# Weight sums of a four-layer attention and SwiGLU kernel as queued steps, in a ring of three groups, with all norms' powers on GpSimd

## The chip, the core and the metric

The kernel runs on one core of a Trainium2 chip. The metric is the device time of one execution in microseconds, and the median of several runs is compared. The kernel before takes 1567.19 us (median of three runs, 1566.94 to 1567.77).

The engines carry the profile's names: PE is TensorE (PEld its weight loads), DVE is VectorE, ACT is ScalarE, POOL is GpSimd, and SP is SyncE, which here only issues transfers. Each engine executes its own instructions strictly in the order in which the program lists them; an instruction that waits for another engine holds up everything behind it.

## The reference

Input x has 2048 tokens of 1024 channels in bfloat16. Two kinds of layer alternate, each twice, and the two layers of a kind share their weights:

```
x = x + A(layernorm(x), wqkv, wo)    # 32 heads of 32; each token attends to 8 tokens, 2 apart, backwards
x = x + B(layernorm(x), w1, w3, w2)  # h = silu(xn @ w1) * (xn @ w3);  out = h @ w2;  F = 3584
x = x + A(...)
x = x + B(...)
```

Layernorm has no weights: (x - mean) / sqrt(var + 1e-5).

## The kernel before

**Units and stages.** The tokens are cut into four chunks of 512. A unit is one chunk in one of the two passes, so there are eight units. First the q, k and v products of the first pass are made for all four chunks (`q_part`), with the attention's scores and values on VectorE beside them. Then `b_stage(u, ...)` runs for each unit: the SwiGLU layer of that chunk, and from unit 1 on also the next pass's q, k and v products of a later chunk.

**Two ways to compute the SwiGLU layer.** Units 0 and 1 (`u < TU`, with `TU = 2`) use ordinary matmuls. The 28 column blocks of F are handled in two splits (16 and 12 blocks), and in groups of four blocks: a group needs one tile of w1 and one of w3, each [128, 8, 512] in bfloat16, 1 MB. For each block, eight matmuls make a gate tile `pg` in PSUM (L1224), ScalarE takes it through Silu to `sg` (L1228), eight more make the up tile `pu` (L1233), and VectorE multiplies the two into `hT` (L1237). After a split comes its w2 stage: eight output tiles `acc` (L1253), added to x by VectorE (L1263). Units 2 to 7 use a seven-product scheme (`products`, L1104 and L1039) that multiplies sums of weight blocks in float16. It spares matmuls, but it needs those sums.

**The weight sums.** They are made once, during units 0 and 1, beside the ordinary matmuls: unit 0 makes those of w1, unit 1 those of w3, and each unit makes half of w2's. For one group of w1 or w3, seven in each unit:

- `measure` (L856): ScalarE squares the whole tile and sums the squares; the squares themselves go to a scratch tile `junk`.
- `scales` (L870): a one-column float32 matmul with a matrix of ones adds the sums over the partitions; four small VectorE steps (L861 to L865) make a power of two out of that.
- `copies` (L883): for each half `a` of the group, four scaled ScalarE copies into a sums buffer. There are two sums buffers, one for each half, both in the tile `big`.
- `differences` (L894): four VectorE subtractions; then GpSimd issues two stores to DRAM (`t_d`, L896 and L897). The buffer is free when those have landed.

`prepare` puts these pieces at fixed places of a group: it is called after each gate tile and each up tile, eight slots in all. Slot 0 measures, slot 4 scales, slots 5 and 7 copy. Parts of w2 go through `transform2` (copies L967, subtractions L972, store L974) at every second output tile of the w2 stage. The sizes of w2 are taken earlier, by `measure2` during the first q, k and v products.

**What sets the order.** The program lists instructions in an order that a planner in the kernel's own code works out while it is built. It keeps a clock for each engine (`now`) and estimates of durations: 0.216 us for a matmul of 512 columns, 7.0 us from the end of the subtractions to a free sums buffer, and for a load 0.45 us of issue, 0.2 us, its kilobytes over 380 and 1.3 us. VectorE's background work lies in queues (`norms`, `makes`, `adds`, `values`, `scores`). `background(until)` lists those steps that fit before a given time. `act_background` does the same for ScalarE with the queues `acts` and `reads`; it takes a step if it would end no later than 2.2 us past TensorE's clock. Small matmuls that wait for VectorE go to `pe_queue`. `pe_requests` takes one when TensorE's clock is 1.5 us past the time at which it is due. `between` calls it once per block.

**The ring.** Weight tiles sit in a ring of six slots of 1 MB (pool `wp`). `seq` lists what goes into them in order, `load_weight` issues the load for the next entry, and `release(n)` with `flush` lets n more entries in. In units 0 and 1 a group takes three entries: w1, w3 and `junk`, which is never loaded. So the ring holds the present group and the next. A group's slots are released when its matmuls are listed (`release(3)` at the group's end).

**The norms.** For the chunks that VectorE normalizes, `norm_stats` takes mean and variance (L233, L236), ScalarE takes Sqrt of the variance (L238, ten times), and VectorE takes its reciprocal (L269) and applies it (L261). For the others `act_norm` does the work on ScalarE, with the power -0.5 on GpSimd (L318 to L324). The ScalarE functions Sqrt, Silu and Exp lie in different tables, and a change of function costs an ACT_TABLE_LOAD.

Of the kernel before, what the change touches and what calls it, by code (L numbers as in the profile page):

```python
# [7 lines left out]
FP32 = mybir.dt.float32  # L8
# [9 lines left out]
def kernel(  # L18
# [186 lines left out]
    nc.gpsimd.memset(ones[:], 1.0)  # L205
    size = const.tile([P, 2, NG], FP32, name="size")
    up_scale = const.tile([P, 2, NG], FP32, name="up_scale")
# [18 lines left out]
    def norm_stats(key, c, r):  # L226

        st = small.tile([P, 2, 2, 6], FP32, name="st")
        mv = small.tile([P, 2, 2], FP32, name="mv", bufs=4)
        sd = small.tile([P, 2], FP32, name="sd", bufs=4)  # L230

        def stats(i, hh):
            nc.vector.bn_stats(st[:, i, hh, :], x_sb[:, c * TPC + 2 * r + i, hh * 512:(hh + 1) * 512])  # L233

        def aggregate(i):
            nc.vector.bn_aggr(mv[:, i, :], st[:, i, :, :])  # L236
            if i == 1:
                nc.scalar.activation(sd[:], mv[:, :, 1], ACTF.Sqrt, bias=epst[:])  # L238
                moments[key, r] = mv, sd, act(0.3, now["dve"] + 0.1, "sqrt")

        for i in range(2):
            for hh in range(2):
                yield 0.61, x_at[c], lambda: stats(i, hh)
            yield 0.12, 0.0, lambda: aggregate(i)

    def norm_apply(key, c, r):
# [4 lines left out]
        free = xnT_free.get(list(xnTs)[list(xnTs).index(key) - 2], 0.0)  # L251
        mv, sd, ready = moments[key, r]
        rstd = small.tile([P, 2], FP32, name="rstd")

# [13 lines left out]

        yield 0.10, ready, lambda: nc.vector.reciprocal(rstd[:], sd[:])  # L269
        for i in range(2):  # L270
            yield 0.47, 0.0 if key[:2] == ("Q", 0) else turned[-3], lambda: apply(i)

# [23 lines left out]

    adds, acts, makes, reads = [], [], [], []

# [58 lines left out]
    def act_background():  # L357
        for queue in (acts, reads):
            while True:
                s = head(queue)  # L360
                if s is None or max(now["act"], s[1]) + s[0] > now["pe"] + 2.2:
                    break
                take_act(queue)
# [318 lines left out]
    for u in range(len(units)):  # L682
        for f0, f1 in fsplits:
# [5 lines left out]
            for g0 in range(f0, f1, FG) if u < TU else ():  # L689
                seq += [("w1", g0, min(FG, f1 - g0)), ("w3", g0, min(FG, f1 - g0)), ("junk", 0, 0)]  # L690
            nq = (f1 - f0) // 2
# [8 lines left out]
    def load_weight(pieces=1):  # L700
# [11 lines left out]
        elif kind == "t2":  # L712
            w = wp.tile([P, 8, 512], FP16, name="t2", tag="w")
            nc.sync.dma_start(w[:, 0:rest[0], :], t2_d[i][:, n])
            at = dma(128 * rest[0], now["pe"])
        elif kind == "junk":
            w = wp.tile([P, KT, FG * P], BF16, name="junk", tag="w")
            at = 0.0
        elif kind in ("early", "late"):
# [9 lines left out]
        else:  # L729
            w = wp.tile([P, KT, FG * P], BF16, name=kind + "t", tag="w")  # L730
            v = w1_v if kind == "w1" else w3_v
            nc.sync.dma_start(w[:, :, 0:n * P], v[:, :, i * P:(i + n) * P])
            at = dma(1200, now["pe"])
        w_at[len(w_tiles)] = at
        w_tiles.append(w)
# [78 lines left out]
    def q_part(l, c, which, ws, then=()):  # L814
# [8 lines left out]
        for t0 in range(0, KT, SG):  # L823
# [17 lines left out]
            nc.sync.dma_start(qkv_d[l][which][:, t0:t0 + SG, c * CH:(c + 1) * CH], sgt)  # L841
            stored = dma(256, done)
            if first and t0 == SG:
                first_at = load_part(qT, 0, 0, 0, False)
            between(False)
            if t0 // SG < len(then) and then[t0 // SG]:
                then[t0 // SG]()
        qkv_at[l, c, which] = stored
        if which == 2:
            xnT_free["Q", l, c] = now["pe"]  # L850
        if first:
            qks[0, 0] = qT, kT, max(done + 0.1, first_at)

    def measure(m, g, w, junk):

        nc.scalar.activation(junk[:], w[:], ACTF.Square, accum_out=size[:, m, g:g + 1])  # L856
        act(3.65)

# [7 lines left out]

    def scales(m, g):

        ps = side.tile([P, 1], FP32, name="size", tag="sd")
        nc.tensor.matmul(ps[:], lhsT=ones[:], rhs=size[:, m, g:g + 1], start=True, stop=True)  # L870
        r = pe(1)
        up, down = up_scale[:, m, g:g + 1], down_scale[:, m, g:g + 1]
        background(r)
        scale_of(ps[:], up, down)
        up_at[0] = dve(0.8, r) + 0.1

    def copies(m, g, w, a):

        settle(a)
        b = blocks[a]  # L880
        KQ = KT // 2
        for i, (kh, fh) in ((0, (0, 0)), (1, (0, 1)), (3, (1, 0)), (5, (1, 1))):
            nc.scalar.activation(b[:, i], w[:, kh * KQ:(kh + 1) * KQ, fh * 256 + a * P:fh * 256 + (a + 1) * P],  # L883
                                 ACTF.Copy, scale=up_scale[:, m, g:g + 1])
        copied.append(act(2.5, max(up_at[0], stored[a])))

    pending = [0, 0]
    copied, stored, up_at = [], [0.0, 0.0], [0.0]

# [9 lines left out]

    def diff_later(m, g, a):  # L900
        pending[a] += 1
        makes.append([differences(m, g, a, copied.pop(0)), None])

    def settle(a):
        force(makes, lambda: not pending[a])

    def prepare(u, g, slot, w1t, w3t, junk):

        w = (w1t, w3t)[u]
        if slot == 0:  # L910
            measure(u, g, w, junk)
        elif slot == 1:
            if g * FG not in [a for a, _ in fsplits]:
                diff_later(u, g - 1, 1)
        elif slot == 4:
            scales(u, g)
        elif slot == 5:
            copies(u, g, w, 0)
        elif slot == 7:
            copies(u, g, w, 1)  # L920
            diff_later(u, g, 0)
            if (g + 1) * FG in [b for _, b in fsplits]:
                diff_later(u, g, 1)

# [4 lines left out]
    def measure2(i, n, at):  # L929

        w = hT[:, 0:n, :]
        for a, b in ((0, n // 2), (n // 2, n)):
            def square():
                nc.scalar.activation(hsum[:].bitcast(BF16).rearrange("p k t -> p (k t)")[:, 0:(b - a) * 512], w[:, a:b, :].rearrange("p k c -> p (k c)"),
                                     ACTF.Square, accum_out=size2[:, len(measured):len(measured) + 1])
                measured.append(i)
            yield (b - a) * 0.45 + 0.2, at, square

    def part_of_w2():

        i = len(w2_parts) - len(unread)
        while len(measured) < 2 * i:
            assert head(reads) is not None
            take_act(reads)
        if unread:
            g0, n, hh = unread.pop(0)
            nc.sync.dma_start(hT[:, 0:n, :], w2_v[:, g0:g0 + n, hh * 512:(hh + 1) * 512])
            reads.append([measure2(i, n, dma(128 * n, now["pe"])), None])

# [11 lines left out]

    def transform2(i, f, ws, loaded):

        settle(f % 2)
        b = big[:, f % 2 * 3584:(f % 2 + 1) * 3584].rearrange("p (b c) -> p b c", b=7)
        for j, (fh, hh) in ((0, (0, 0)), (2, (0, 1)), (1, (1, 0)), (5, (1, 1))):
            nc.scalar.activation(b[:, j], ws[hh][fh][:, f, :], ACTF.Copy, scale=up2[:])  # L967
        r = act(2.5, max(loaded, stored[f % 2]))

        def rest():  # L970
            for out, x, y in ((4, 5, 2), (2, 2, 0), (3, 5, 2), (6, 1, 3)):
                yield 0.46, r, lambda: nc.vector.tensor_tensor(b[:, out], b[:, x], b[:, y], op=ALU.subtract)  # L972
            pending[f % 2] -= 1
            nc.gpsimd.dma_start(t2_d[i][:, :, f, :], b)  # L974
            stored[f % 2] = now["dve"] + 7.0

        pending[f % 2] += 1
        makes.append([rest(), None])

    def scale_h():  # L980
# [215 lines left out]
    def b_stage(u, hold):  # L1196
# [7 lines left out]
        for (f0, f1) in fsplits:  # L1204
# [4 lines left out]
            for g0 in range(f0, f1, FG):  # L1209
                gn = min(FG, f1 - g0)  # L1210
                w1t, w3t, junk = weight("w1"), weight("w3"), weight("junk")
                for fi in range(gn):
# [16 lines left out]
                    ts = act(0.5, r, "silu")  # L1229
                    prepare(u, g0 // FG, 2 * fi, w1t, w3t, junk)  # L1230
                    pu = bank("pu")
# [6 lines left out]
                    th = dve(0.64, r)  # L1238
                    prepare(u, g0 // FG, 2 * fi + 1, w1t, w3t, junk)
                release(3)  # L1240
            if lastsplit:
                xnT_free["B", l, c] = now["pe"]
            split, nq = fsplits.index((f0, f1)), (f1 - f0) // 2
            flush()
            got = [(weight("w2", False), w_at[used[0] - 1]) for _ in range(4)]
            tiles, times = [[[got[2 * hh + fh][i] for fh in range(2)] for hh in range(2)] for i in range(2)]
            for hh in range(2):
                now["pe"] = max(now["pe"], *times[hh])
                for j in range(TPC):
# [7 lines left out]
                    r = pe(1, th)  # L1257
                    if step % 2 == 0 and step < nq:
                        transform2(split, (step + u * nq) // 2, tiles, times[1][1])
                    background(r + 1.0)  # L1260
                    dve(0.64, r)
                    xs = x_sb[:, n, hh * 512:(hh + 1) * 512]
                    nc.vector.tensor_tensor(xs, xs, acc[:], op=ALU.add)  # L1263
                    if j == TPC - 1 and hh == 1:
                        release(4)
                    between(hold and not lastsplit, lastsplit and hh == 0 and j == 1 and not hold)
        if u == TU - 1:
            force(makes, lambda: not makes)
            scale_h()
# [81 lines left out]
```

## Time and profile before

| what | value |
|---|---|
| median of three runs | 1567.19 us |
| the profiled execution: time | 1569.21 us |
| the profiled execution: span, first to last instruction | 1567.5 us |
| mean granted TensorE clock | 0.996 |
| busy: PE, DVE, ACT, POOL | 1541.4, 1193.0, 928.7, 109.4 us |
| units 0 and 1, about 200 to 536 us: PE, DVE, ACT, POOL busy | 327.9, 290.9, 216.9, 42.3 us of 336 |
| moved by DMA | 431 MB, mean 275 GB/s |

A time in a view counts from the start of the span. "L870" is line 870 of the kernel, whose functions are printed above. In a group's row, `out<-in` names the tiles, `xcount` counts instructions, and after the bar stand total busy time and mean duration. "Idle before" is how long the engine stood before such an instruction, and the name behind the arrow is what ended that. In the windows, PEclk is the share of the full clock that TensorE was granted; at 0.50 every matmul takes twice as long. The ends of matmuls are modelled, so the start times tell more than the busy share.

### The profile page before, as it was taken

The page shows a single profiled execution, that of the slowest core. Times are in us where ns is not written, and L with a number is a line of the kernel's source. Part 1 is how long each engine was busy: PE and PEld are TensorE (multiplying, and loading weights), DVE is VectorE, ACT ScalarE, POOL GpSimd, SP SyncE. Part 2 cuts the span into 40 slices and gives each one's busy share as a digit, 9 for nine tenths or more (in the row PEclk, how much of TensorE's full clock was granted, in tenths as well). Part 3 has the DMA queues.
Part 4 walks back from the last instruction along what each step waited for, and adds up shares of the span by engine and source line. Part 5 has one row for each costly group of instructions (what it writes and reads, how often), then busy time and mean ns, then how long its engine had stood idle before and what let it go on. Part 6 is the DMA issues. An engine that isn't in the chain of part 4 may idle for free.

```text
span 1567.5 us, 25163 instructions
## 1 busy us (share of the span) xinstructions
PE 1541.4 (98%) x9730; PEld 997.1 (64%) x9730; DVE 1193.0 (76%) x2058; ACT 928.7 (59%) x1445; POOL 109.4 (7%) x227
## 2 busy tenths in 40 slices
PE   9999999999799999999999999999999999999999
PEld 7666644444344568585676857767677667776866
DVE  4789988988878889897889865897378985445345
ACT  4786577575857436565556754756648355644634
POOL 0111001011111100000001010000201000000000
PEclk9999999999999999999999999999999999999999
DMA  9667769697969796988869788797978977978885
GB/s 323 194 186 220 223 196 335 207 342 244 268 235 341 234 308 246 321 277 296 277 244 313 291 281 271 274 328 264 319 271 284 327 269 253 319 276 325 319 293 207
DMA packets 258359, 431.17 MB, mean 275 GB/s; under 512 B 72832, under 2 KB 200064, under 8 KB 241984
## 3 DMA queue, kind: packets, MB, share of 16 engines
q1 hardware_dynamic: 248464, 390.90, 75.2%
q0 software_dynamic: 9632, 38.54, 6.3%
q8 instruction: 76, 1.25, 0.3%
q14 instruction: 43, 0.35, 0.1%
q10 hardware_dynamic: 144, 0.13, 0.0%
HBM read 345.90 MB, written 67.90 MB: 264 GB/s over the span
## 4 chain that ended last, share of the span: by engine, by line
PE 55%; DVE 8%; ACT 2%; DMA 1%; issue 1%; ACTq 0%; DVEq 0%
PE st L1104 29%; PE w L1039 13%; PE ps L830 8%; PE po L772 4%; DVE tree L668 1%; DVE tree L504 1%; DMA t_d<-big 1%; DVE tree L584 1%; DVE hT L1010 1%; DVE hT L1122 1%; DVE x_sb L1024 0%; PE pe L639 0%; DMA xnT<-xn 0%; DVE big L289 0%; ACT sg L1113 0%
## 5 line engine op out<-in xcount | busy, mean ns | idle before, releaser
L830 PE MATMUL ps<-xnT,wqkv 128*128 128x512 f16 (+1 forms) x1472 | 321.4, 379 | 0.0
L1104 PEld LDWEIGHTS <-early 128*128 128x128 f16 x2688 | 263.5, 98 | 42.4 <-issue 3.1
L830 PEld LDWEIGHTS <-wqkv 128*128 128x128 bf16 x1472 | 210.8, 144 | 108.3 <-issue 1.7
L1039 PE MATMUL w<-t,hT 128*128 128x512 f16 x1008 | 226.1, 379 | 2.2 <-ACT big L1059 1.8
L1104 PEld LDWEIGHTS <-late 128*128 128x128 f16 x2016 | 197.0, 98 | 32.5 <-issue 2.9
L584 DVE TENSOR_TENSOR tree<-qT,kT 128x2048 bf16<-128x2048 bf16 x128 | 156.2, 1221 | 35.7 <-DMA kT<-qkv_d 17.4
L504 DVE TENSOR_TENSOR tree<-tree 128x1024 bf16<-128x1024 bf16 x256 | 175.0, 684 | 0.8
L1104 PE MATMUL st<-xnT,late 128*128 128x256 f16 x1344 | 174.2, 273 | 1.1 <-ACT big L1142 1.1
L1104 PE MATMUL st<-big,early 128*128 128x256 f16 x1344 | 173.8, 274 | 1.2 <-ACT sg L1113 1.1
L1039 PEld LDWEIGHTS <-hT 128*128 128x128 f16 x1008 | 98.1, 98 | 115.2 <-issue 3.2
L1104 PE MATMUL st<-xnT,early 128*128 128x256 f16 x1344 | 166.0, 273 | 0.0
L668 DVE TENSOR_TENSOR tree<-At,vT 128x2048 bf16<-128x2048 bf16 x128 | 156.1, 1219 | 10.8 <-ACT At L641 9.7
L772 PE MATMUL po<-wo,oT 128*128 128x512 bf16 x512 | 116.2, 379 | 2.0 <-DVE x_sb L777 2.0
L1133 ACT COPY st<-st 128x512 f32<-128x512 f32 x84 | 48.5, 577 | 111.5 <-PE st L1104 107.2
L1233 PE MATMUL pu<-xnT,w3t 128*128 128x512 f16 x448 | 107.5, 383 | 0.0
L1224 PE MATMUL pg<-xnT,w1t 128*128 128x512 f16 x448 | 107.0, 382 | 0.1
L834 ACT CAST hT<-ps 128x512 bf16<-128x512 f32 x96 | 56.0, 586 | 84.6 <-PE ps L830 83.7
L1145 DVE TENSOR_TENSOR st<-st,big 128x512 f32<-128x512 f32 x84 | 58.4, 695 | 56.4 <-ACT big L1142 56.2
L1253 PE MATMUL acc<-w2t,hT 128*128 128x512 bf16 x448 | 98.5, 379 | 0.0
L1113 ACT ACTIVATE sg<-st,down_scale 128x512 bf16<-128x512 f32 x126 | 86.6, 688 | 12.3 <-PE st L1104 12.0
L772 PEld LDWEIGHTS <-oT 128*128 128x128 bf16 x512 | 50.0, 98 | 59.0 <-issue 3.5
L1104 PE MATMUL st<-big,late 128*128 128x256 f16 x672 | 87.1, 273 | 0.0
(172 smaller groups left out, 1932.3 us busy)
## 6 DMA issues: line engine op xcount, KB each, us to landing
early<-t_d SPq DMA_DIRECT2D x84, 1024.0 KB, 6.5
late<-t_d SPq DMA_DIRECT2D x84, 768.0 KB, 6.2
t<-t_d SPq DMA_DIRECT2D x42, 1024.0 KB, 6.6
t<-t_d SPq DMA_DIRECT2D x42, 768.0 KB, 4.9
wqkv<-in_A_wqkv_dram SPq DMA_DIRECT2D x28, 1024.0 KB, 7.1
w1t<-in_B_w_dram SPq DMA_DIRECT2D x14, 1024.0 KB, 7.7
w3t<-in_B_w_dram SPq DMA_DIRECT2D x14, 1024.0 KB, 9.8
t_d<-big POOLq DMA_DIRECT2D x28, 512.0 KB, 6.5
```

The costliest lines, as they stand in the source:

```text
L504: nc.vector.tensor_tensor(b, b, buf[:, 4:8, :], op=ALU.add)
L584: V.tensor_tensor(pr, qT[:], kT[:, :, k0:k0 + TCH], op=ALU.mult)
L668: V.tensor_tensor(tm, At[:], win, op=ALU.mult)
L772: nc.tensor.matmul(ps[:], lhsT=oT[:, t, j * P:(j + 1) * P], rhs=wo[:, t, hh * 512:(hh + 1) * 512], start=(t == 0), stop=(t == KT - 1))
L830: nc.tensor.matmul(ps[:], lhsT=ws[kk // KH][:, kk % KH, t::KT], rhs=xnT[:, kk, :], start=(kk == 0), stop=(kk == KT - 1))
L1039: nc.tensor.matmul(out[:], lhsT=lhs[:, k, j * P:(j + 1) * P], rhs=w[:, k, :], start=start and k == 0, stop=k == nq - 1, skip_group_check=True)
L1104: nc.tensor.matmul(out[:, a, :], lhsT=w[:, a, blk, k, :], rhs=rhs[:, k, :], start=start and a == 0 and k == 0, stop=k == KQ - 1, skip_grou ...
L1113: nc.scalar.activation(sg[:], src, ACTF.Silu, scale=inv)
L1145: nc.vector.tensor_tensor(G["D"][:], G["D"][:], su, op=ALU.add)
L1224: nc.tensor.matmul(pg[:], lhsT=w1t[:, kk, fi * P:(fi + 1) * P], rhs=xnT[:, kk, :], start=(kk == 0), stop=(kk == KT - 1))
L1233: nc.tensor.matmul(pu[:], lhsT=w3t[:, kk, fi * P:(fi + 1) * P], rhs=xnT[:, kk, :], start=(kk == 0), stop=(kk == KT - 1))
L1253: nc.tensor.matmul(acc[:], lhsT=hT[:, f, j * P:(j + 1) * P], rhs=tiles[hh][f // nq][:, f % nq, :], start=(f == 0), stop=(f == f1 - f0 - 1))
```

## The change

- **No scratch slot.** `junk` leaves the ring. The squares go to `hsum`, which is idle until unit 2. Six slots now hold three groups of w1 and w3.
- **Measuring from the landing on.** When `load_weight` lists the load of the tile whose sums are to be made (w1 in unit 0, w3 in unit 1), it queues the generator `weight_size` on a new ScalarE queue, `parts`, and `weight_sums` on `reads`. `act_background` looks at `acts`, `parts` and `reads` in this order. The squares are made in two halves of 2048 columns, due when the planner expects the tile. The two size matmuls become a request in `pe_queue`, due 0.3 us after the planned end of the second half, and the four scale steps a step in `makes`.
- **Copies as single steps.** The eight copies of a group are steps of 0.61 us, due when the scale is there and the sums buffer is expected to be free. After four of them the subtractions are queued. `act_background` is called after each Silu and at each output tile of the w2 stage, where `prepare` and `transform2` stood.
- **Held tiles.** A group's two slots are released once its sums' copies are listed. `release_held(keep)` forces this for the oldest groups until `keep` are left: one at a group's start and end, none at the third output tile of the w2 stage. In the w2 stage the copies of w2 (`sums_of_w2`) must be listed before its four tiles are released.
- **Norms.** The ten Sqrt on ScalarE and the ten reciprocals on VectorE become two GpSimd steps each: add 1e-5, then the power -0.5.

The diff, cut to its core:

```diff
-                nc.scalar.activation(sd[:], mv[:, :, 1], ACTF.Sqrt, bias=epst[:])
-                moments[key, r] = mv, sd, act(0.3, now["dve"] + 0.1, "sqrt")
+                nc.gpsimd.tensor_scalar(rstd[:], mv[:, :, 1], EPS, None, op0=ALU.add)
+                nc.gpsimd.tensor_tensor(rstd[:], rstd[:], powers[:], op=ALU.pow)
+                moments[key, r] = mv, rstd, now["dve"] + 2.0
...
-        yield 0.10, ready, lambda: nc.vector.reciprocal(rstd[:], sd[:])
...
-        for queue in (acts, reads):
+        for queue in (acts, parts, reads):
...
-                seq += [("w1", g0, min(FG, f1 - g0)), ("w3", g0, min(FG, f1 - g0)), ("junk", 0, 0)]
+                seq += [(kind, g0, min(FG, f1 - g0), (u, g0 // FG) if m == u else None)
+                        for m, kind in enumerate(("w1", "w3"))]
...
             at = dma(1200, now["pe"])
+            if rest[0]:
+                got = {}
+                parts.append([weight_size(*rest[0], w, at, got), None])
+                reads.append([weight_sums(*rest[0], w, got), None])
...
+    def weight_size(m, g, w, at, got):
+
+        w_ = w[:].rearrange("p k c -> p (k c)")
+        half = w_.shape[1] // 2
         up, down = up_scale[:, m, g:g + 1], down_scale[:, m, g:g + 1]
+        for i in range(2):
+            yield 1.95, at, lambda: nc.scalar.activation(junk, w_[:, i * half:(i + 1) * half], ACTF.Square,
+                                                         accum_out=size[:, m, g, i:i + 1])
...
+        def add_up(t):
+            ps = side.tile([P, 1], FP32, name="size", tag="sd")
+            for i in range(2):
+                nc.tensor.matmul(ps[:], lhsT=ones[:], rhs=size[:, m, g, i:i + 1], start=i == 0, stop=i == 1)
+            makes.append([scale_item(ps, pe(2, t)), None])
+
+        t = now["act"] + 0.3
+        pe_queue.append((lambda: t, lambda: add_up(t)))
+
+    def weight_sums(m, g, w, got):
+
+        while "at" not in got:
+            yield "blocked"
         KQ = KT // 2
+        for a in range(2):
+            while pending[a]:
+                yield "blocked"
+            pending[a] += 1
+            b = blocks[a]
+            for i, (kh, fh) in ((0, (0, 0)), (1, (0, 1)), (3, (1, 0)), (5, (1, 1))):
+                c0 = fh * 256 + a * P
+                yield 0.61, max(got["at"], stored[a]), lambda: nc.scalar.activation(
+                    b[:, i], w[:, kh * KQ:(kh + 1) * KQ, c0:c0 + P], ACTF.Copy,
+                    scale=up_scale[:, m, g:g + 1])
+            makes.append([differences(m, g, a, now["act"] + 0.1), None])
+        made.add((m, g))
...
+    def finish_sums(done):
+
+        while not done():
+            if head(reads) is not None:
+                take_act(reads)
+            elif head(parts) is not None:
+                take_act(parts)
+            elif head(makes) is not None:
+                take(makes)
+            else:
+                pe_requests(1, True)
+
+    def release_held(keep):
+
+        while held and (len(held) > keep or held[0] in made):
+            key = held.pop(0)
+            finish_sums(lambda: key in made)
+            release(2)
...
-                w1t, w3t, junk = weight("w1"), weight("w3"), weight("junk")
+                w1t, w3t = weight("w1"), weight("w3")
+                release_held(1)
...
-                    prepare(u, g0 // FG, 2 * fi, w1t, w3t, junk)
+                    act_background()
...
-                    prepare(u, g0 // FG, 2 * fi + 1, w1t, w3t, junk)
-                release(3)
+                    release_held(2)
+                held.append((u, g0 // FG))
+                release_held(1)
...
-                    if step % 2 == 0 and step < nq:
-                        transform2(split, (step + u * nq) // 2, tiles, times[1][1])
+                    if step == 2:
+                        release_held(0)
+                    if step == 0:
+                        steps = range(u * nq // 2, (u + 1) * nq // 2)
+                        reads.extend([sums_of_w2(split, f, tiles, max(times[0] + times[1])), None] for f in steps)
+                    act_background()
```

## The prediction

> **What bounds the kernel now.** I read the page's table of slices first.
>
> ```profile
> span 1567.5 us, 25163 instructions
> ...
> PE   9999999999799999999999999999999999999999
> ...
> PEclk9999999999999999999999999999999999999999
> ```
>
> TensorE is busy in every slice but one, and its clock is full: the kernel is bound by TensorE's own instruction stream. An edit on another engine pays only where TensorE stands still. The page gives 1541.4 of 1567.5 us busy, so all standstill together is 26 us, spread over the run. Next, the view of waits for TensorE alone says what it stood for:
>
> ```profile
> PE size L870 <- ACT junk L856: 8.0, 1, 8.0
> PE L L597 <- DVE psm L508: 4.8, 2, 2.6
> PE po L772 <- DVE x_sb L777: 2.0, 2, 1.1
> ```
>
> The columns are total, times, longest. One wait is far the largest: the one-column matmul that adds up a weight tile's squares (L870) stood 8.0 us for the ScalarE Square (L856). It is one event out of fourteen groups. The windows around it:
>
> ```profile
> 415.00:420.00 5.00, 4.91 (x24) 2.04 (x21) 1.61 (x4) 3.10 (x5) 0.00 (x0) 1.00 0.97 339
> 420.00:425.00 5.00, 0.23 (x2) 0.00 (x0) 4.86 (x8) 4.97 (x8) 1.07 (x2) 0.90 1.10 360
> 425.00:430.00 5.00, 1.80 (x6) 0.98 (x7) 4.86 (x11) 4.12 (x4) 1.07 (x2) 0.50 1.06 388
> 430.00:435.00 5.00, 5.00 (x15) 1.84 (x14) 2.54 (x6) 2.56 (x4) 0.00 (x0) 0.57 1.04 377
> ```
>
> After the window and its length come PE, PEld, DVE, ACT and POOL busy, then the granted clock. The standstill costs twice: 8 us idle, then a clock of 0.50 until 434, with 15 matmuls where 24 or 25 fit. Why ScalarE was late is in its timeline:
>
> ```profile
> 413.27 1.95 ACT L883 ACTIVATE big<-w3t,up_scale 128x512 f16<-128x512 bf16 x3 [3.47 <-DMA t_d<-big]
> 417.08 0.72 ACT L883 ACTIVATE big<-w3t,up_scale 128x512 f16<-128x512 bf16 x1 [1.87 <-DMA t_d<-big]
> ...
> 424.44 3.61 ACT L856 ACTIVATE junk<-w3t 128x4096 bf16<-128x4096 bf16 x1
> ```
>
> Copies of the previous group stood in ScalarE's queue for a store of the sums buffer to land; the Square of this group was queued behind them and behind three table loads, and TensorE behind the Square.
>
> **What the change removes.** (a) Stall. Eight matmuls of one tile follow at 1.725 us (the starts 409.45 and 411.18 in the timeline), so the one after 418.34 was due at 420.07. It started at 428.65, of which about 0.13 is the size matmul itself: 8.45 us lost. At half clock, 428.65 to the next up tile at 434.87 is 6.22 us for 16 matmuls that take 3.45: 2.77 lost. Together **-11.2**. Now the Square is queued when the tile lands, a group earlier, and the size matmul is a request that TensorE takes only when the planner's clock is 1.5 us past the Square's planned end plus 0.3. ScalarE's copies still wait for stores; what is late next is the gate's own drain, and that has room: PSUM has six buffers in this pool, two per pair of tiles, so three pairs or 10.3 us pass before TensorE lacks one.
>
> (b) A second standstill lies downstream, 578.55 to 580.79, for score sums that VectorE made late:
>
> ```profile
> 575.00:580.00 5.00, 3.55 (x21) 2.38 (x20) 4.93 (x8) 1.74 (x3) 0.00 (x0) 1.00 0.40 140
> 580.00:585.00 5.00, 4.21 (x27) 2.67 (x27) 2.17 (x5) 0.69 (x2) 0.00 (x0) 0.66 0.90 256
> ```
>
> It costs 2.24 us and, at half clock, 24 matmuls in 4.13 us instead of 2.6: 3.7 in all. The chain of waits leads from it back over VectorE (4.93 of 5 us busy) to a transposing transfer at 550.78 (5.28 us), the norm at 526.16, the table load and Sqrt at 524.34 to 525.93 and the copies (L967) at 522.39, which stood for a store of the sums (513.44, 8.9 us). Those steps come earlier, and the norm no longer passes ScalarE. Bounds 0 and -3.7; nothing says how far VectorE's later queue gives it back, so I take half, **-1.9**.
>
> **What it adds.** (c) Each of 14 groups gets a second size matmul. In the timeline a pair of instructions (one fp32 matmul) moves the next tile from 214.465 to 214.60: 0.135 us. 14 x 0.135 = **+1.9**, on TensorE's own path, certain.
>
> (d) A new dependence: the Square now waits for the load, which before had always landed. If it is late, ScalarE's queue stands, and the size matmul, and TensorE, with everything behind it. The planner prices the first tile of a pair at 0.45 + 0.2 + 1200/380 + 1.3 = 5.1 us and the second at 8.3. In the DMA view, six pairs issued on their own landed after 5.2, 5.1, 9.1, 6.6, 8.0, 5.9 and 9.8, 8.4, 14.4, 8.9, 9.9, 6.4. Only three of the twelve exceed the price by more than the guard of 1.8: by 2.2, 1.1 and 4.3, mean 0.63 over twelve. Requests are looked at once per pair of tiles (3.45 us), on average 1.7 us after they come due; that leaves 0.5, 0 and 2.6, mean 0.26. 14 x 0.26 = **+3.6** (ends 0 and 14 x 0.63 = 8.9).
>
> (e) Hidden on ScalarE: two half Squares instead of one. The nearest row, 128x2048 at 1911 ns plus a read of 191 ns, against 3608 + 192: 28 x 2.1 - 14 x 3.8 = +5.6 us. Against that, 10 Sqrt at 0.30 and 7 table loads at 1.28 go, -12.0, and some return loads. ScalarE is 216.9 of 336 us busy from 200 to 536: nothing on the path. VectorE loses 10 reciprocals at 0.155 (1.6 us of 290.9). The copies and subtractions keep number and size; a busier ScalarE without slack would show them in the gate's drain.
>
> (f) GpSimd gets an add and a power per norm, by its rows 0.23 + 0.72 = 0.95 us (maxima 1.10 + 1.54). They replace load, Sqrt and reciprocal, 1.28 + 0.30 + 0.16 = 1.74: -0.8 us of latency at the medians, +0.9 at the maxima. GpSimd's issues of stores stand ahead in its queue, but wait only for VectorE steps ahead of the same bn_aggr. Transposes and sums lie behind; 0 in the sum. The Trainium skill, "SBUF — State Buffer", section "SBUF: two separate sides", speaks against this: GpSimd shares a port pair with VectorE, and a VectorE operation with two SBUF inputs shuts out a GpSimd read for its whole length. The rows show such stretching (medians 0.23 and 0.72, maxima above). If each of the ten norms came one 1.2 us operation later by that rule, none would reach TensorE and the sum would stand.
>
> (g) The ring. Six slots hold three groups instead of two and two scratch slots. A load now waits for ScalarE's last copy of a group, and SP's queue (transposes, scores' loads) behind it. Before, the same slots came free at the end of the group, so the next load has the same 13.8 us. The median landing is 8.6, leaving 5.2; without that cover the maximum of 16.4 would show as 2.6 us. Taken as 0.
>
> Clock and short waits: the gap of 2.24 us at 578.55 halved the clock, while 2.5 us at 60.5 left it at 1.00. "TensorE: Matmul & The Clock Gate", "Part 1: The HAM clock gate", lets the clock fall after an idle window of some 3.4 us. By that (d)'s waits would cost no clock; by the row at 580 one of them could add 1.5 us. The measured gap shows that the short waits are not always free.
>
> **Sum.** -11.2 - 1.9 + 1.9 + 3.6 = -7.6. The profiled execution took 1569.21 us, 1.7 outside its span and 2.0 over the median of 1567.19; the difference is set against the median: **1559.6**. With (b) full and (d) zero, -13.0: 1554.2; with (b) zero and (d) 8.9, -0.4.
>
> **Rivals.**
> 1. The stall only moves. The wait for stores stays: at 7.0 us after the subtractions the planner is optimistic (issues 0.54 + 0.54, then a median of 7.4 to landing, about 8.5). Against it: thirteen of fourteen size matmuls never waited, with no guard. If one of 14 waits 8 us again, -11.2 returns: 1564 to 1570, about 1567.
> 2. Slower: late Squares stop TensorE in every group. Place: the size request; price: the median landing of all 28 loads, 8.6, is 3.5 over 5.1, less the guard 1.8 = 1.7 a group, x 14 = 24. 1567.2 - 11.2 + 1.9 + 24 = 1582. It decides from (11.2 - 1.9)/14 = 0.66 us a group. For it: the measured tile is the one whose slot ScalarE's copies hold, and store traffic (38.5 MB) isn't in the planner's loads. Against it: loads issued singly met the price.
> 3. The change acts and all that was hidden comes too: 1554, inside my range.
>
> **Chances.** Forecast (1553 to 1564, with rival 3) 0.59, rival 1 0.14, rival 2 0.27 (1571 to 1595). The range 1553 to 1577 leaves out some 0.02 below and 0.15 above. A measurement of this kernel tells 0.2%, 3.1 us, from no change: faster 0.59, same 0.14, slower 0.27.
>
> **What would show it.** Right: no L870-like wait over 1 us, clock 1.00 from 415 to 435, size matmuls 56 records instead of 28, no Sqrt in ScalarE. Step (b): the gap before the first scores matmul of the product stage. Wrong: waits of TensorE for the Square in several groups, ScalarE waiting for DMA w1t or w3t, gate tiles waiting for weights after a w2 stage, or GpSimd rows above 2 us with xnT late.

## The result, and the profile after

| | before | after |
|---|---|---|
| median of four runs each, on one chip | 1567.07 us (1562.1 to 1567.77) | 1601.5 us (1599.96 to 1602.9) |
| span of the profiled execution | 1567.5 us | 1601.2 us |
| PE, DVE, ACT, POOL busy | 1541.4, 1193.0, 928.7, 109.4 us | 1551.5, 1192.9, 915.8, 125.8 us |

The ratio is 1.0226, 95% interval [1.0202, 1.0251]: the change made the kernel 34 us slower. The forecast was 1559.6 in 1553 to 1577, with 0.59 on faster. The span grew by 33.7 us. Of these, 23.6 are standstill of TensorE (span less its busy time: 26.1 before, 49.7 after). The other 10.1 lie in its busy time: 2.9 for 28 more size matmuls (7.1 against 4.2 us), and the rest goes with the lower mean clock (0.990 against 0.996).

The page's table of slices, after:

```profile
span 1601.2 us, 25179 instructions
...
PE   9999979998998989999999999999999999999999
...
PEclk9999989999999999999999999999999999999999
```

A slice is 40 us. The dents lie in slices 6 to 15, that is from 200 to 600 us, where units 0 and 1 run and the sums are made. The waits of TensorE (total, times, longest):

```profile
PE po L773 <- DVE x_sb L778: 10.5, 6, 4.7
PE L L596 <- DVE psm L507: 8.3, 3, 4.5
PE size L969 <- ACT hsum L948: 7.8, 1, 7.8
PE pg L1243 <- ACT sg L1247: 4.3, 1, 4.3
PE pu L1252 <- DMA w3t<-in_B_w_dram: 1.5, 1, 1.5
```

The wait that the prediction was about, the size matmul of a weight tile (L870 before, L883 now), is gone; all its 56 records together waited 0.1 us. In its place stand several others. The first is at 200 us, where the first q, k and v products end. ScalarE's timeline there:

```profile
200.36 0.59 ACT L835 CAST big<-ps 128x512 bf16<-128x512 f32 x1 [1.14 <-PE ps L831]
200.84 1.91 ACT L871 ACTIVATE hsum<-w1t 128x2048 bf16<-128x2048 bf16 x1
...
202.88 1.91 ACT L871 ACTIVATE hsum<-w1t 128x2048 bf16<-128x2048 bf16 x1
...
204.91 1.48 ACT L948 ACTIVATE hsum<-hT 128x1536 bf16<-128x1536 bf16 x1
...
206.52 1.48 ACT L948 ACTIVATE hsum<-hT 128x1536 bf16<-128x1536 bf16 x1
```

w2's size matmul (L969) must have the last two w2 Squares (L948). They stand in the same first-in, first-out queue `parts` behind the two new Squares of group 0 (L871), whose tile had landed (they wait for nothing). TensorE stood 7.82 us, until 208.15. Yet ScalarE had been idle 1.14 us before each of the last three evacuations (the bracket in the first line). A half Square takes 1.91 us, so behind an evacuation it makes the next one late, and the planner does not list it there: it is planned at 1.95 us, the evacuation at 0.5 behind TensorE's clock, and the window of 2.2 us does not hold both. So both halves were left over until the last w2 Squares were forced out of the queue. In kernel 17 below, with a wider window, they stand between the evacuations from 180.76 on, and TensorE waited for nothing there.

From there on the sums run late. The copies' rows give first and last start:

```profile
L883 ACT ACTIVATE big<-w1t,up_scale x56: 704/708/722, 215.6 to 343.1; 128x512 f16<-128x512 bf16 x56
L883 ACT ACTIVATE big<-w3t,up_scale x56: 704/708/722, 372.8 to 510.3; 128x512 f16<-128x512 bf16 x56
```

These two are before; after it is:

```profile
L901 ACT ACTIVATE big<-w1t,up_scale x56: 704/712/762, 229.3 to 367.7; 128x512 f16<-128x512 bf16 x56
L901 ACT ACTIVATE big<-w3t,up_scale x56: 705/712/722, 411.9 to 544.3; 128x512 f16<-128x512 bf16 x56
```

Number and duration agree. The w1 copies begin 13.7 us later and the last starts 24.6 us later, in the w2 stage of their split, where the copies of w2 have to come too. At the first group most of the delay does not come from the Squares: its size matmul started at 217.01, 2.6 us later than before (214.46), but the four scale steps behind it stood in VectorE's queue until 228.28, 11.3 us, where they had started 0.4 us behind it before. What the late sums do is seen around 480 us:

```profile
464.95 5.01 ACT L901 ACTIVATE big<-w3t,up_scale 128x512 f16<-128x512 bf16 x8 [3.75 <-DVE up_scale L863]
476.54 1.91 ACT L871 ACTIVATE hsum<-w3t 128x2048 bf16<-128x2048 bf16 x1 [6.58 <-DMA w3t<-in_B_w_dram]
...
480.48 5.00 ACT L984 ACTIVATE big<-w2t,up 128x512 f16<-128x512 bf16 x8
489.99 2.56 ACT L984 ACTIVATE big<-w2t,up 128x512 f16<-128x512 bf16 x4 [4.51 <-DMA t_d<-big]
493.36 2.56 ACT L984 ACTIVATE big<-w2t,up 128x512 f16<-128x512 bf16 x4 [0.81 <-DMA t_d<-big]
495.82 1.54 ACT L1247 ACTIVATE sg<-pg 128x512 bf16<-128x512 f32 x3
```

Read it downwards. The last group's copies end at 470, so its slots come free and the load of the next w3 tile goes out at 469.98. The Square of that tile is already listed, and ScalarE stands 6.58 us for it. Behind it come sixteen copies of w2, eight of which stand again for stores; behind those the first Silu of the next split, whose gate tile was begun at 481.58 and which starts only at 495.82. TensorE, having begun three pairs of tiles since 481.58, had no PSUM buffer left, stood 4.34 us and then ran at half clock:

```profile
496.45 3.57 PE L1243 MATMUL pg<-xnT,w1t 128*128 128x512 f16 x8 [4.34 <-ACT sg L1247]
```

```profile
485.00:490.00 5.00, 5.00 (x25) 2.26 (x24) 2.27 (x6) 0.49 (x2) 1.81 (x2) 1.00 0.57 233
490.00:495.00 5.00, 2.10 (x10) 0.88 (x9) 2.30 (x5) 4.19 (x7) 0.09 (x1) 1.00 0.35 138
495.00:500.00 5.00, 3.55 (x9) 1.28 (x9) 3.35 (x5) 2.36 (x5) 0.80 (x1) 0.50 0.88 253
500.00:505.00 5.00, 4.43 (x17) 1.57 (x14) 2.12 (x5) 1.13 (x2) 0.00 (x0) 0.82 1.02 368
```

TensorE ran 10, 9 and 17 matmuls where 25 fit. A like loss ends at 393.56. Copies of w2, held up by a store, stand ahead of two Silus (388.46). The products that need these, and w2's subtractions, stand on VectorE ahead of an addition to x (L778), for which TensorE waits 4.68 us; the clock is 0.57 from 392 to 400. Around 570 us TensorE itself waits only 0.97 us, for an evacuation behind w2's last copies. But w2's subtractions wait for these copies too, and behind the subtractions stands a norm (L261, 573.89): its transposed x comes late, VectorE stands 10.46 us for it, and TensorE 4.46 us, until 595.20, for score sums (L507).

### The profile page after: what moved, and what is told of

It is laid out like the page before. It is cut to its first block, busy times and chain, and to the rows that moved or that the text cites. A ratio compares the mean times of both kernels' runs of the same rounds, so it can differ in the third digit from the quotient of the medians.

```text
span 1601.2 us, 25179 instructions
## 1 busy us (share of the span) xinstructions
PE 1551.5 (97%) x9712; PEld 1002.2 (63%) x9758; DVE 1192.9 (75%) x2048; ACT 915.8 (57%) x1452; POOL 125.8 (8%) x247
## 4 chain that ended last, share of the span: by engine, by line
PE 70%; DVE 13%; DMA 8%; ACT 6%; issue 2%; SPq 1%; POOL 0%; ACTq 0%; DVEq 0%; POOLq 0%
PE st L1122 28%; PE w L1057 13%; PE ps L831 12%; PE po L773 6%; PE pg L1243 4%; PE pu L1252 4%; DMA t_d<-big 3%; DVE tree L583 2%; PE acc L1274 2%; DVE tree L503 2%; DMA w3t<-in_B_w_dram 1%; DVE tree L667 1%; DMA x_sb<-in_A_x_dram 1%; DMA kT<-qkv_d 1%; ACT big L901 1%
```

## The experiments

Kernels are numbered as in their labels (there is no kernel 4); each is compared with the kernel before on the same chip. The kernel before took 1565.35 to 1567.95 us on the five chips of these runs, so kernels from different chips are compared by their ratios. The first four expectations were written when the main theory was that the loss lies only in the order of listing at the forced points, each by itself.

**Kernels 1 and 2: one part alone.** The norms alone are the diff's norm lines on the kernel before. The ring alone:

```diff
-  ("w1", ...), ("w3", ...), ("junk", 0, 0)
+  ("w1", ...), ("w3", ...)          # six slots hold three groups
-  activation(junk[:], w[:], Square, accum_out=size[:, m, g:g + 1])
+  for i in range(2): activation(hsum half, w half i, Square, accum_out=size[:, m, g, i:i + 1])
   # two size matmuls; all at the old fixed slots
```

> The kernel before with one part of the change: the ten norms take their power on GpSimd. Theory 1 (the loss is the order in which ScalarE's steps are listed: w2's size squares behind a weight tile's squares, and w2's copies ahead of the next split's Silu): the norms are innocent, 1560 to 1569 us. Theory 2 (GpSimd's powers come late, shut out by VectorE, and the transposed x with them): at least 1577.

> The kernel before with one part of the change: no scratch slot, so a ring of three groups; squares in two halves to the idle tile, two size matmuls, all at the old fixed places. Theory 1: the ring is innocent; +1.9 us for the matmuls and 0 to -11 for the one old stall, 1558 to 1570. Theory 3 (the deeper ring makes transfers collide, and loads wait for slots): at least 1577.

Norms alone: 1564.72, ratio 0.9995 [0.9985, 1.0005], in the range of theory 1. Ring alone: 1574.35, ratio 1.0051 [1.0035, 1.0066], between the ranges of theories 1 and 3. The norms cost nothing that could be measured, the ring with halved Squares some 8 us. Neither holds the 34 us; the rest of the change is the queue.

**Kernels 3 and 5: one forced place alone.** w2's size steps in a queue of their own ahead of `parts`; and, separately, w2's copies forced only in the second block of the next group (at three of four split ends).

```diff
-        for queue in (acts, parts, reads):
+        for queue in (acts, first, parts, reads):
-            parts.append([measure2(...), None])
+            first.append([measure2(...), None])
```

> The changed kernel, with the squares of w2's parts in a queue of their own ahead of the weight tiles' squares. Theory 1: the standstill of 7.8 us before w2's size matmul at 200 us goes, with its half clock (about 9 us) and perhaps the standstill for x at 221 (4 us): 1586 to 1594. Theories 2 and 3: 1598 to 1603, since neither has to do with that queue.

> The changed kernel, but the copies of w2's sums need not be listed by the end of the w2 stage; they are forced only after the second block of the next group, and w2's tiles are released then (three of the four split ends; the last one as before). Theory 1: the standstills at 389 to 400 and 492 to 501 us shrink, as the next split's Silu no longer stands behind copies that wait for stores: 1580 to 1592. Against it (the stores and the late loads are the limit, wherever the copies are listed): 1597 or more, with gate matmuls that wait for weights.

1598.75, ratio 1.0207 [1.0192, 1.0222], and 1600.2, ratio 1.0214 [1.0198, 1.023]: theory 1 missed both, and both times lie in its rivals' ranges. In the first the 7.8 us at 200 are gone, but TensorE waits 14.0 us for a cast of the scores (At) at 481 us, 8.8 for an evacuation and 6.9 for a Silu. In the second it waits 16.0 us for w1 and w3 tiles, since late copies hold the slots; such waits are what the rival to theory 1 named. The loss moves, so the order at either of these places alone is not the whole cause.

**Kernels 6, 7, 9 and 10: w1's and w3's sums against w2's.** Three theories now. **A**: the sums of w1 and w3 begin too late. **B**: the queued, forced copies of w2 are at fault. **C**: two sums buffers, each free only when its stores have landed, cannot carry the work at all. Four kernels: w2's copies back at every second output tile, with the last group of w1 or w3 finished at the first (6); the ring-alone kernel with only w2's copies queued (7); the sums brought forward (9); and 6 and 9 together (10). The edits of 9, beside the `first` queue above:

```diff
-  ... > now["pe"] + 2.2
+  ... > now["pe"] + (2.7 if queue is parts else 2.2)     # a half Square fits
-  makes.append([scale_item(ps, pe(2, t)), None])
+  r = pe(2, t); background(r); scale_of(ps[:], up, down); got["at"] = dve(0.8, r) + 0.1
-  while "at" not in got:
+  while "at" not in got or not sized:    # no copy into big before the first products are done
```

> The changed kernel, but the copies of w2's sums stand again at every second output tile of the w2 stage (four listed together), and the last group of w1 or w3 is finished at the first of them; the sums of w1 and w3 stay queued steps. Theory A, the sums of w1 and w3 run late from the first group on (a half Square of 1.95 us does not fit the planner's window, the scale steps lie behind other VectorE steps, about 14 us later than before at group 0): the late groups still stand ahead of the w2 stage, so 1594 to 1603. Theory B, the queued w2 copies, forced at the end of the w2 stage ahead of the next Silus, are what stops TensorE (388 us, 492 us): 1580 to 1588. Theory C, two sums buffers cannot carry this work in the time there is: within 3 us of 1600.

> The ring-alone kernel (1574.35: sums of w1 and w3 at their fixed places, ring of three groups, halved Squares) with only the copies of w2's sums as queued steps, finished at the end of the w2 stage. Theory A: near the ring-alone kernel, 1572 to 1578. Theory B: 1583 to 1592. Theory C: the same buffers do the same work, so no more than 3 us from the ring-alone kernel unless the forced end lies differently.

> The changed kernel with everything of w1's and w3's sums brought forward: w2's size steps ahead of the Squares, the window for a Square 2.7 us in place of 2.2 (so it fits between two evacuations), the scale steps listed right after the size matmul, and the copies held back only until the first products are done. The w2 copies stay queued and forced as in the change. Theory A: the standstills at 200, 388 and 492 us go, 1570 to 1580. Theory B: only the one at 200 us goes, 1592 to 1599. Theory C: the groups start early but catch up with the buffers' stores again, 1592 to 1600.

> The kernel of the early sums (w2's sizes first, wider window for Squares, scale steps at once), and w2's copies at the fixed places of before. Theories A and B both: 1562 to 1575, at or under the ring-alone kernel's 1574. Theory C: 1588 or more, with copies that wait for stores ahead of the w2 stages.

| | w2's copies queued | w2's copies at fixed places |
|---|---|---|
| w1 and w3 queued as in the change | 1601.5, 1.0226 [1.0202, 1.0251] | (6) 1592.9, 1.0164 [1.0149, 1.0179] |
| w1 and w3 queued, brought forward | (9) 1588.73, 1.0131 [1.0116, 1.0146] | (10) 1571.26, 1.0026 [1.0017, 1.0036] |
| w1 and w3 at fixed slots | (7) 1566.36, 1.0001 [0.9989, 1.0013] | (2) 1574.35, 1.0051 [1.0035, 1.0066] |

Kernels 6 and 9 fell between the ranges of A and B, kernel 7 below both, and kernel 10 into the range of both together. C falls: kernel 7 makes the same sums in the same two buffers in the time of the kernel before. B alone falls too: in the last row a queue for w2's copies costs nothing, and is even 8 us faster than the fixed places. It costs 17 us where w1's and w3's sums are queued as well and early. Why, the timeline of kernel 9 shows, first ScalarE's (L904 copies w3, L988 copies w2), then the tile of TensorE that waited for the Silu:

```profile
363.70 5.01 ACT L904 ACTIVATE big<-w3t,up_scale 128x512 f16<-128x512 bf16 x8 [7.68 <-DVE up_scale L863]
372.14 5.00 ACT L988 ACTIVATE big<-w2t,up 128x512 f16<-128x512 bf16 x8 [3.44 <-DMA t_d<-big]
381.50 2.56 ACT L988 ACTIVATE big<-w2t,up 128x512 f16<-128x512 bf16 x4 [4.36 <-DMA t_d<-big]
383.97 1.54 ACT L1251 ACTIVATE sg<-pg 128x512 bf16<-128x512 f32 x3
...
384.59 3.57 PE L1247 MATMUL pg<-xnT,w1t 128*128 128x512 f16 x8 [7.57 <-ACT sg L1251]
```

The eight copies of w3 belong to the *next* unit's first group. They entered `reads` with the load, before the w2 stage was reached, and so went ahead of w2's copies, which are due at the end of the stage. These then had to wait for both buffers' stores, ahead of the Silu. Theory **D**: the queue serves first what came first, not what is due first.

**Kernels 8, 11, 12 and 13: the scale steps, and the order.** Scale steps at once on the change (8) and on kernel 6 (11); kernel 9 with w2's copies ahead (12); and, for a faster kernel, 7 with the size matmul at slot 5 and the copies at slots 6 and 7 (13). The edit of 12:

```diff
-  if step == 2: release_held(0)
+  if step == 0: release_held(0)
-  reads.extend([sums_of_w2(...), None] for f in steps)
+  reads[0:0] = [[sums_of_w2(...), None] for f in steps]
-  while "at" not in got or not sized:
+  while "at" not in got or not sized or not prior <= made:   # prior: w2's sums of the split before
```

> The changed kernel; only the four VectorE scale steps of a group are listed right behind its size matmul, as before, and not queued behind the subtractions. The runs so far: queued w2 copies cost nothing where w1's and w3's sums keep their places (1566.4), and fixed w2 copies alone save 8.6. Theory A1, the queued scale steps are what makes the sums of w1 and w3 late (the copies of the last group waited 5.6 us for up_scale at 363 us and 3.8 us at 465 us): 1580 to 1590, with the standstill at 200 us left. Theory A2, the Squares that do not fit the window are what makes them late: 1597 to 1603.

> The kernel with w2's copies at fixed places (1592.9), and the scale steps at once. Theory A1: 1572 to 1582, that is the early sums with fixed w2 copies (1571.3) and up to 11 us for the standstill at 200 us and the one behind it. Theory A2: 1588 to 1595.

> The kernel of the early sums (1588.7, all queued), but w2's copies stand ahead of the next group's copies in the queue: the last group is finished at the first output tile of the w2 stage, and the next group's copies wait until w2's are made. Theory D, in the early kernel the next group's copies, in the queue since the landing of its tile, went ahead of w2's (363.7 against 372.1 us) and so made w2's run into the next Silus: the 7.6 us of a gate tile for a Silu at 382 us goes, 1568 to 1577. Rival: two sums buffers and their stores hold the w2 copies back whichever stands first, 1584 to 1592.

> The kernel with only w2's copies queued (1566.4; it still has 3.0 us of TensorE waiting for the Squares at 425 us, with the clock at half for a while), and in each group the size matmul one place later (slot 5 of 8 in place of 4) and the copies at slots 6 and 7 in place of 5 and 7. Theory: the size matmul of the kernel before stood a little too early for one busy group, and a place later (1.7 us) pays for the standstill: 1559 to 1563, under the kernel before. Rival: copies so near the group's end run into the next group's Silus and the w2 stage, 1567 to 1575.

Kernel 8: 1598.16, ratio 1.0208 [1.0187, 1.023]. Kernel 11: 1588.4, 1.0147 [1.0131, 1.0162]. Both lie in the range of A2. So A1 falls: although the scale steps make up most of the delay of the first group, listing them at once gains only some 3 us of 34, by the ratios (1.0226 to 1.0208 and 1.0164 to 1.0147), with intervals that overlap. Kernel 12: 1565.04, ratio 0.9998 [0.9988, 1.0007], by the ratios 21 us under kernel 9 and below even the range of D; the rival is out, and D holds. Its timeline in the same stage (L992 copies w2, L908 copies w3):

```profile
340.26 5.00 ACT L992 ACTIVATE big<-w2t,up 128x512 f16<-128x512 bf16 x8
...
353.62 2.55 ACT L992 ACTIVATE big<-w2t,up 128x512 f16<-128x512 bf16 x4
365.10 0.60 ACT L1255 ACTIVATE sg<-pg 128x512 bf16<-128x512 f32 x1 [8.93 <-PE pg L1251]
366.28 0.72 ACT L908 ACTIVATE big<-w3t,up_scale 128x512 f16<-128x512 bf16 x1 [0.58 <-DMA t_d<-big]
```

Now w2's copies are done 9 us before the Silu, which waits for TensorE and not the other way round. Kernel 13: 1560.65, ratio 0.9964 [0.9954, 0.9974], in the range of its theory and under the kernel before.

**Kernels 14 to 17: which of the three counts.** w2 ahead alone (14), with the scale steps at once (15), with the early start (17); and kernel 12 with the size matmul asked for 4 us later (16: `t = now["act"] + 4.3` in place of 0.3).

> The changed kernel with w2's copies ahead of the next group's, nothing else. Theory D, the order in which the queue holds w2's copies and the next group's is the main defect: 1576 to 1588, with the 13 us around 200 us left. Theory E, the sums start so late that there is no next group's copy to go ahead of (in the changed kernel the last group's own copies come first, at 363 us): 1594 to 1602, and worse than that where the last group is forced earlier.

> The changed kernel with w2's copies ahead and the scale steps at once, without the early start (Squares in the old window, w2's sizes behind them). Theory D: 1574 to 1582, the kernel with all three (1565.0) and the standstill at 200 us with what follows it. Theory E: the late start alone keeps the w2 stages late, 1586 to 1598.

> The kernel with all three without the scale steps at once: they stand in the queue behind the subtractions again. If order and start are what counts: 1563 to 1570. If the scale steps are a condition too: 1576 to 1590, with copies of a last group waiting for up_scale at a w2 stage.

> The kernel with all three (1565.0; TensorE stood 4.6 us for Squares, and the clock fell to half around 450 us), with the size matmul asked for 4 us later. Theory: the queue's last price is this guard, 1556 to 1562. Rival: sums that come 4 us later bring the w2 copies back into the next Silus, 1567 to 1580.

| kernel | us | ratio |
|---|---|---|
| 14: w2 ahead | 1585.16 | 1.0121 [1.0106, 1.0136] |
| 15: w2 ahead, scale at once | 1588.53 | 1.0152 [1.0121, 1.0184] |
| 17: w2 ahead, early start | 1567.12 | 1.0000 [0.9984, 1.0016] |
| 12: w2 ahead, early start, scale at once | 1565.04 | 0.9998 [0.9988, 1.0007] |
| 16: 12, size request 4 us later | 1585.15 | 1.0120 [1.0105, 1.0135] |

Kernel 14 is in the range of D, 15 in that of E (a late start is enough to keep the w2 stages late), so both act. Kernel 17, with both, is in the range of "order and start are what counts". The scale steps have no steady sign: some 3 us faster in 8 and 11, no difference in 12, 3 slower in 15. Kernel 16 was meant to be faster and lost 19 us, and is above both ranges of its expectation: where everything else is in order, a size matmul asked for 4 us later brings back more than half of the loss. At 459.18 its ScalarE stood 12.07 us for a w3 tile, and sixteen w2 copies followed, the pattern of 476.54 above.

**Kernels 18 and 19: what was left.** w2's sizes first and w2 ahead, the window as in the change (18); and kernel 13 with the GpSimd norms (19).

> The changed kernel with w2's copies ahead (1585.2 alone) and w2's size steps ahead of the Squares, but with the window for a Square as in the change. If what counts at the start is only which of the Squares stands in front at the forced point: 1564 to 1573, as the kernel with the wider window too (1567.1). If a Square has to find room between the first products' evacuations: 1576 to 1590.

> The fastest kernel so far (w1's and w3's sums at fixed slots with the size matmul at slot 5, ring of three groups, w2's copies queued, 1560.65) and GpSimd powers for all norms. The norms alone moved the kernel before by less than can be measured (ratio 0.9995), so 1558 to 1563; if ten Square roots and table loads less on ScalarE help where the copies stand close: 1553 to 1557.

Kernel 18: 1579.04, ratio 1.0081 [1.0061, 1.0101], in the range of "a Square has to find room". Its first Square of a weight tile starts at 205.42, that of kernel 17 at 180.76. So, by the ratios and in this order, w2 ahead saves 16 us (1.0226 to 1.0121), w2's sizes first 6 (to 1.0081), room for a half Square 13 (to 1.0000), and the scale steps nothing clear (to 0.9998), which is 36 us together. In another order the shares differ: brought forward first, the early sums save 15 (to 1.0131) and w2 ahead then 21. Kernel 19: 1558.93, ratio 0.9944 [0.9927, 0.996], in the range for norms that cost nothing, the fastest here: the ring and the norms of the change, w2's copies queued, but w1's and w3's sums at fixed slots. Its small step from kernel 13 is not shown, as the two intervals overlap. A third sums buffer was not tried. What of "w2 ahead" is the order and what the last group's earlier end was not separated.

## Why the prediction was wrong

The failed step is the one that had no term. Under (e) it says "The copies and subtractions keep number and size; a busier ScalarE without slack would show them in the gate's drain". They did keep both, and ScalarE became *less* busy (928.7 to 915.8 us). What changed was when the planner lists them. A fixed slot finishes a group's copies inside the group; the queue takes a step only where it fits a window, in the order of arrival, and makes up for it at forced points, ahead of a Silu or an evacuation. I costed each operation and took the queue for at least as early as the slot. Its copies began 13.7 us later at the first group and the last of w1's started 24.6 us later. With the order and the start put right the same queue takes the time of the kernel before (kernel 12, 0.9998), so this missing term is the loss of 34 us.

- **(a)** The stall went, as said. "What is late next is the gate's own drain" named the right wait. "That has room", 10.3 us, was measured against one late operation; the gate tile begun at 481.58 got its Silu 14.2 us later, behind sixteen copies of w2 and the stores that these waited for. The step failed in what stands ahead of the drain, not in the size of the room.
- **(b)** Wrong sign: the waits of the L matmul for VectorE's score sums grew from 4.8 to 8.3 us, and the one of this term from 2.24 to 4.46. In kernel 12, where the sums are on time, only 1.2 us near 60 us is left: the chain was read rightly, its input was late.
- **(c)** Right in kind and too small: 56 records, 7.1 us busy for 4.2. One size matmul moves the next tile by 0.135 us, two by 0.36, as at 481.22. That adds 0.23 a group and 3.2 us in all, where +1.9 was taken.
- **(d)** The place was wrong for the change (0.1 us at the request). Where ScalarE waited for a tile (9.2 us for w3t in all), the price was paid by the w2 copies and Silus behind it. In kernel 12 the mechanism does appear, once. ScalarE's Square waited 10.55 us for its tile, and TensorE for the Square:

```profile
445.00:450.00 5.00, 3.33 (x16) 1.46 (x14) 0.00 (x0) 3.53 (x4) 0.00 (x0) 1.00 0.01 4
450.00:455.00 5.00, 2.10 (x6) 1.01 (x7) 4.29 (x6) 5.00 (x8) 0.00 (x0) 0.72 0.00 0
455.00:460.00 5.00, 5.00 (x15) 1.90 (x14) 4.69 (x14) 2.60 (x5) 0.90 (x1) 0.60 0.30 123
```

  37 matmuls where 75 fit at 25 a window: 38/75 of 15 us, 7.6 us lost, inside the bounds of 0 and 8.9 but above the +3.6 taken. With this, (b) full and (c) as measured, -11.2 - 3.7 + 3.2 + 7.6 = -4.1; kernel 12 measured -0.3 (1565.04 against 1565.35 on its chip). So the sum describes the change with the queue in the right order to some 4 us; for the change as made it lacked the largest term.
- **(f)** Right: the norms alone measured 0.9995. GpSimd's add and power had medians of 0.232 and 0.718 us, maxima of 1.081 and 0.881. The rule that GpSimd and VectorE shut each other out of a shared port pair (the Trainium skill, "SBUF — State Buffer", "SBUF: two separate sides") shows at most in these few maxima. VectorE waited for a norm's power once, 0.6 us, and TensorE never.
- **(g)** Right about TensorE in the change itself (1.5 us for w3t), but for a reason that does not hold in general: the cover of 5.2 us is as long as the copies are early. Kernel 5 holds the slots longer and waits 16.0 us for tiles.

The second rival had the right sign for a wrong reason: it put the loss at the size request, which waited 0.1 us, and its range, 1571 to 1595, ends below the measured time. Of the signs listed as "wrong", ScalarE's wait for w3t was there, and one wait of 1.5 us for weights after a w2 stage, of an up tile and not a gate tile; what stands behind ScalarE's wait had no price.

## What to carry to other kernels

When a step moves from a fixed place to a queue, price its *time* and not only its work: for the first instance, ask whether the step fits the window that it is offered at all; at each forced point, write down which steps stand ahead of the one that is forced, and what waits behind them. A queue that serves by arrival must not hold work with different deadlines. And where two fixes each give less than half, try them together before dropping the theory: here w2 ahead alone saved 16 us and the early sums alone 15, both together 36.

## What the runs showed of the hardware

- Short gaps can cost clock, and not all do. Gaps of TensorE of 2.24 us (before, 578.55), 2.30 (after, until 221.56; 0.50 from 222 to 225) and 2.60 (kernel 17, until 481.01; 0.66 in that window) were followed by a lower clock, gaps of 0.78 and 1.51 (after, 404.29 and 505.94) were not, nor was 2.5 at 60.5 before. The idle window of some 3.4 us that the Trainium skill gives ("TensorE: Matmul & The Clock Gate", "Part 1: The HAM clock gate") would have spared the first three; the measured gaps decide.
- A stall costs more than its length. After, at 492 us: 4.34 us of standstill; from 490 to 505, 36 matmuls where 75 fit, 7.8 us lost, though shorter waits in these windows are in it. In kernel 12, at 453 us: 4.6 us of standstill, 7.6 lost. Before, at 420 us: 8.45 and 11.2. That is some 3 us more than the standstill each time.
